# Bulk loads from ScalarE's queue instead of SyncE's, and raw tiles loaded and searched one product later

## The chip, the cores and the metric

The kernel runs on one core of a Trainium2 chip. Its engines are TensorE (PE in the profile; PEld is its weight load), VectorE (DVE), ScalarE (ACT), GpSimd (POOL) and SyncE (SP), which only issues transfers. An engine takes its instructions in order and waits for semaphores of the others. A transfer is issued by an instruction of SyncE, ScalarE or GpSimd and moved by 16 DMA engines. The metric is the device time of one execution in microseconds.

## What is computed

Two independent parts, whose results stand side by side in the output: a causal attention with a sliding window of 256 (2048 tokens, 32 heads of 32), and an FNet mixing layer, the real part of a two-dimensional DFT written as products with DFT matrices.

```
def _A_ref(x, wqkv, wo):
    H = 32; Dh = D // H; W = 256
    q, k, v = ...
    scores = jnp.einsum("bhqd,bhkd->bhqk", q, k) * (Dh ** -0.5)
    mask = (idx[:, None] - idx[None, :] >= 0) & (idx[:, None] - idx[None, :] < W)
    p = _softmax(jnp.where(mask[None, None], scores, -1e9), axis=-1)
    ...
    return o @ wo
def _B_ref(x, dft_seq_re, dft_seq_im, dft_hid_re, dft_hid_im):
    a = jnp.einsum("bsd,ed->bse", x, dft_hid_re)
    b = jnp.einsum("bsd,ed->bse", x, dft_hid_im)
    return jnp.einsum("ts,bse->bte", dft_seq_re, a) - jnp.einsum("ts,bse->bte", dft_seq_im, b)
```

## The kernel before

All inputs are float32. To multiply them on TensorE in float16, each tile is scaled by a power of two and split into a high and a low half; a product of two split tiles is three passes of matmuls (`PASSES`). The scale comes from a search over the raw tile (its largest value, or a sum of absolute values), and a small matmul (`pt_...`, L183) spreads the result over the partitions.

**Stages.** First the projections q, k and v (matmuls pq, pk, pv of 128x512), whose results go to a scratch tensor in HBM (qk, vs). From about 140 us on, the attention runs between the matmuls of everything else: 256 blocks of 128 queries, each with scores (s, far), an exponential on ScalarE (L278), a split (L281, L282), a DMA transpose on SyncE (L284), and the product with v (pv). The generator `attention` is stepped by `tick`, at a rate given by tables, so the attention is spread evenly over the matmuls.

From about 565 us on come four rounds of 12 units. In a round the first four units ("x") multiply the DFT over the hidden axis: their left operand lies in HBM as ready sums and differences (xs), which `x_left` loads as un_a, un_b, un_c and a quarter "t" into `spare`, a part of reg1. The other eight units ("c") multiply the DFT matrix of the sequence axis: `u_load` loads two raw float32 tiles (raw_u, 512 KB each), `u_top` searches them on ScalarE (L786), `u_scale` spreads the scale (pt_u), and `u_step` splits and combines them into un_a, un_b, un_c and a part of reg1. A unit is one call of `seven`: a Strassen-like scheme with seven products of 12 matmuls, accumulated in three PSUM banks in the order "abacaba". After product 0 ScalarE copies bank a to bank c (L1084); after the others ScalarE copies a bank out (L1053) or VectorE adds it (L1055). Names p_a, p_b, p_c are these banks. The last stage multiplies the attention's output with wo (po_a, po_b, po_c).

**What sets the order.** The program is written out in one order; a scheduler then orders each engine's instructions by the times it expects, and `tc.issue_after(i)` forbids it to put an instruction before i on the same engine. In the rounds, `do(n, turn, f, ...)` puts work of later units behind product `turn` of unit n. `behind_act[0]` is ScalarE's latest copy out of PSUM, `behind[0]` the latest of VectorE's. Raw tiles rotate through 5 buffers (`rawp`), un_a, un_b, un_c through 4 (`stp`), the attention's qk tiles through 2.

**Loads.** Every load goes out from SyncE, in one line with the stores and the transposes. `do_load` (L230) loads the q and k of one group and chunk of the attention, two blocks before a chunk ends, or at its first use. `u_load` (L777; the first two units of a round go through `load`, L216) loads the raw tiles of unit n behind products 1 and 5 of unit n - 3; `u_top` searches them behind products 0 and 2 of unit n - 2, `u_scale` follows behind product 6. `x_left` (L806, L811) loads the left sums of unit n behind products 0, 3 and 4 of unit n - 1.

Of the kernel before, what the change touches and what calls it, by code (L numbers as in the profile page):

```python
# [15 lines left out]
AF = mybir.ActivationFunctionType  # L16
# [37 lines left out]
def fused_kernel(ctx: ExitStack, tc: tile.TileContext, xa, wqk, wv, wo, xb, wd, cs, out):  # L54
# [92 lines left out]

    marks = []

    def top(key, raw, i, n):  # L150

        if i == 0:
            tops[key] = small.tile([P, n], F32, tag=f"top{n}", name=f"top_{key}")
        with tc.issue_after(behind[0].ins) if behind else nullcontext():
            vec(nc.vector.tensor_reduce, tops[key][:, i:i + 1], raw, axis=AX.XY, op=ALU.max,
                apply_absolute_value=True)

    def mean(key, raw, i, n):
# [59 lines left out]
    def attention():  # L218
# [6 lines left out]

        def do_load(g, hp, sc):
            if (g, hp, sc) in q2s:
                return
            u = att.tile([96, 2, 2, CH], F16, tag="qk", name=f"qk_{g}_{hp}_{sc}")
            nc.sync.dma_start(u.rearrange("p h a t -> p (h a t)"), qk[g, sc, :, :, 2 * hp:2 * hp + 2]  # L230
                              .rearrange("j d h a t -> (j d) (h a t)"))
            q2s[g, hp, sc], k2s[g, hp, sc] = u[:, :, 0], u[:, :, 1]
# [10 lines left out]
        def s_step(b, j):  # L243
# [33 lines left out]
            for h in range(2):  # L277
                nc.scalar.activation(sv[:, h], sv[:, h], AF.Exp, bias=bias[:, h:h + 1], scale=es)  # L278
            hl = att.tile([P, 8 * P], F16, tag="hl", bufs=3, name=f"hl_{b}")
# [72 lines left out]
        for b in range(nblk + LAG):  # L352
            for j in range(2):
# [16 lines left out]
                if j == 1 and b < nblk and blocks[b][3] == 1 and b + 3 < nblk:  # L370
                    g, hp, sc, _ = blocks[b + 3]
                    if (g, sc) in ready:
                        do_load(g, hp, sc)
                if j == 1 and b < nblk and blocks[b][3] == 3 and b + 1 < nblk:
# [398 lines left out]
    def u_load(n, j=0):  # L773
        if n < len(units):
            kind, p, c, i = units[n]
            raws[n, j] = rawp.tile([P, ND, P], F32, tag="raw", name=f"raw_u{n}_{j}")
            (load if i < 2 else nc.sync.dma_start)(raws[n, j], cs[p, 2 * i + j, :, 8 * c:8 * c + 8])  # L777

# [19 lines left out]
    def x_left(n, step):  # L798

        _, _, c, k = units[n]  # L800
        src = xs[4 * c + k]
        u = uns.setdefault(n, {})
        part = lambda t, k0: (lambda h, d: t[:, h, k0 + d])
        if step == "t":
            t = spare[:, k % 2 * 8 * P:(k % 2 + 1) * 8 * P]
            nc.sync.dma_start(t, src[:, 6 * HP:])  # L806
            u[5] = part(t.rearrange("p (h k t) -> p h k t", h=2, k=4), 0)
            return
        j, held_by = {"a": (0, (0, 3)), "c": (1, (6, 4)), "b": (2, (2, 1))}[step]
        t = stp.tile([P, 2, ND, P], F16, tag="st", name=f"un{n}_{step}").rearrange("p h d t -> p (h d t)")  # L810
        nc.sync.dma_start(t, src[:, 2 * j * HP:2 * (j + 1) * HP])  # L811
        for k, pos in enumerate(held_by):
            u[pos] = part(t[:, k * HP:(k + 1) * HP].rearrange("p (h d t) -> p h d t", h=2, d=4), 0)
# [292 lines left out]
    with tc.tile_pool(name="pb", bufs=1) as pb:  # L1106
# [14 lines left out]
        for r in range(4):  # L1121
# [8 lines left out]
            for j in range(8):  # L1130
                n = c0 + j
                do(n - 3, 1, u_load, n, 1)
                do(n - 3, 5, u_load, n, 0)
                do(n - 2, 0, u_top, n, 1)
                do(n - 2, 2, u_top, n, 0)
                do(n - 2, 6, u_scale, n)
                for step, turn in enumerate((0, 1, 1, 2, 3, 4)):
                    do(n - 1, turn, u_step, n, step)
# [125 lines left out]
```

## Time and profile before

| | us |
|---|---|
| median of three runs (1696.62 to 1700.1) | 1697.67 |
| profiled execution | 1697.51 |
| its span, first to last instruction | 1695.7 |

The busy time of every engine in 40 equal slices of the span (tenths; 9 is 90% or more), the mean busy share of the 16 DMA engines, and below it the part of the page on DMA queues:

```profile
PE   9999999999999999999999999999999999999999
PEld 4444545554555554555554555545555545444444
DVE  7657888888888689887688896688886698687442
ACT  4476666677877687887687886687887688563322
POOL 0000222334434341444423475433565425411000
DMA  6678999999999994887998999986999977866431
...
q1 hardware_dynamic: 462064, 321.48, 75.9%
q0 software_dynamic: 7680, 25.17, 9.0%
```

A row of a group of instructions reads: line, engine, operation, what it writes, what it reads, how often, busy time, mean duration in ns, idle time before it and what ended that. A row of waits reads: who waited for whom, total us, times, longest us.

### The profile page before, as it was taken

To read this page: it belongs to the slowest core of one execution; us is meant where nothing else is said; L and a number is where in the kernel's file an instruction comes from. 1 tells how busy PE (TensorE), PEld (TensorE's weight loads), DVE (VectorE), ACT (ScalarE), POOL (GpSimd) and SP (SyncE) were. 2 spreads that over 40 slices of the span, in tenths; PEclk is the share of its full clock that TensorE was granted. 3 is DMA by queue.
4 is the path that set the end of the run, shared out by engine and by line. 5 is a ranking of instruction groups with operands and counts; after the bars stand their busy time and mean duration, and the time that the engine had idled before them with its cause. 6 is when DMAs were issued, how large, how long until landed. Compare 5 with 4: busy or idle time off the path is not lost.

```text
span 1695.7 us, 30919 instructions
## 1 busy us (share of the span) xinstructions
PE 1687.6 (100%) x11007; PEld 846.6 (50%) x11007; DVE 1304.8 (77%) x2256; ACT 1169.8 (69%) x2035; POOL 571.0 (34%) x812
## 2 busy tenths in 40 slices
PE   9999999999999999999999999999999999999999
PEld 4444545554555554555554555545555545444444
DVE  7657888888888689887688896688886698687442
ACT  4476666677877687887687886687887688563322
POOL 0000222334434341444423475433565425411000
DMA  6678999999999994887998999986999977866431
GB/s 246 239 269 246 248 289 285 279 259 303 245 234 222 208 225 122 205 200 171 232 245 250 196 182 182 230 200 120 193 183 203 227 181 140 174 184 120 116 99 75
DMA packets 469898, 348.62 MB, mean 206 GB/s; under 512 B 376944, under 2 KB 409968, under 8 KB 468848
## 3 DMA queue, kind: packets, MB, share of 16 engines
q1 hardware_dynamic: 462064, 321.48, 75.9%
q0 software_dynamic: 7680, 25.17, 9.0%
q8 instruction: 86, 1.41, 0.3%
q14 instruction: 68, 0.56, 0.1%
HBM read 166.99 MB, written 106.17 MB: 161 GB/s over the span
## 4 chain that ended last, share of the span: by engine, by line
PE 83%; ACT 4%; DMA 4%; DVE 3%; issue 3%; POOL 2%; SPq 0%; POOLq 0%; ACTq 0%; DVEq 0%
PE p_a L119 23%; PE pv L119 12%; PE p_b L119 11%; PE pk L119 9%; PE pq L119 9%; PE p_c L119 6%; PE po_a L119 5%; PE s L119 3%; PE po_b L119 2%; PE far L119 1%; PE po_c L119 1%; DMA o<-ohl 1%; POOL z L296 1%; ACT s L278 1%; POOL t L298 1%
## 5 line engine op out<-in xcount | busy, mean ns | idle before, releaser
L278 ACT ACTIVATE s<-s,bias,escs 128x256 f32<-128x256 f32 (+1 forms) x512 | 270.1, 528 | 11.7
L296 POOL TENSOR_SCALAR_AFFINE_SELECT z<-t 128x512 f16<-128x512 f16 x224 | 183.1, 825 | 190.0 <-PE pv L119 167.2
L275 POOL TENSOR_SCALAR bias<-bias 128x1 f32<-128x1 f32 x128 | 53.5, 418 | 548.0 <-ACT bias L272 405.3
L272 ACT ACTIVATE bias<-mx,pshift,escs 128x2 f32<-128x2 f32 x256 | 98.4, 384 | 165.4 <-DVE mx L269 164.4
L282 DVE TENSOR_TENSOR hl<-s,hl 128x512 f16<-128x512 f32 (+1 forms) x256 | 169.8, 664 | 50.4 <-ACT hl L281 49.9
L119 PEld LDWEIGHTS <-reg 128*128 128x128 f16 x1344 | 128.7, 97 | 141.6
L298 POOL TENSOR_SCALAR_AFFINE_SELECT t<-t 128x512 f16<-128x512 f16 x224 | 188.1, 848 | 11.6
L119 PE MATMUL p_a<-reg,un_c 128*128 128x512 f16 x768 | 181.4, 379 | 0.5 <-DVE reg L859 0.3
L119 PE MATMUL pk<-reg,wu_k 128*128 128x512 f16 x768 | 174.3, 379 | 0.0
L269 DVE TENSOR_REDUCE mx<-s 128x2 f32<-128x512 f32 (+1 forms) x256 | 170.7, 667 | 3.4
L119 PE MATMUL pv<-reg,reg 128*128 128x512 f16 x768 | 172.5, 379 | 0.0
L119 PEld LDWEIGHTS <-un_c 128*128 128x128 f16 x1152 | 109.9, 97 | 121.8 <-issue 2.4
L119 PEld LDWEIGHTS <-un_b 128*128 128x128 f16 x1152 | 109.4, 97 | 117.4 <-issue 0.7
L119 PEld LDWEIGHTS <-un_a 128*128 128x128 f16 x1152 | 109.4, 97 | 116.5
L119 PE MATMUL pq<-reg,wu_q 128*128 128x512 f16 x696 | 156.3, 379 | 0.0
L281 ACT ACTIVATE hl<-s 128x512 f16<-128x512 f32 (+1 forms) x256 | 148.8, 581 | 5.5
L119 PE MATMUL p_a<-reg,un_b 128*128 128x512 f16 x576 | 136.4, 379 | 0.1
L119 PE MATMUL p_c<-reg,un_a 128*128 128x512 f16 x576 | 136.5, 379 | 0.0
L119 PE MATMUL p_b<-reg,un_b 128*128 128x512 f16 x576 | 136.3, 379 | 0.1
L119 PE MATMUL p_a<-reg,un_a 128*128 128x512 f16 x576 | 136.2, 379 | 0.0
L267 DVE COPY_PREDICATED s<-upper,far 128x256 f32<-128x256 uint32 x224 | 94.3, 421 | 51.6 <-PE s L119 50.6
L119 PEld LDWEIGHTS <-qk 96*128 96x128 f16 x1056 | 87.6, 97 | 63.6 <-DMA qk<-qk 2.2
(217 smaller groups left out, 3136.6 us busy)
## 6 DMA issues: line engine op xcount, KB each, us to landing
raw_u<-in_cs_dram SPq DMA_DIRECT2D x64, 512.0 KB, 4.8
qk<-qk SPq DMA_DIRECT2D x64, 384.0 KB, 4.8
out_dram<-y POOLq DMA_DIRECT2D x72, 256.0 KB, 6.2
raw_wd<-in_wd_dram SPq DMA_DIRECT2D x24, 512.0 KB, 5.6
vs<-yv SPq DMA_DIRECT2D x32, 264.0 KB, 4.1
vt<-vs SPq DMA_DIRECT2D x64, 132.0 KB, 3.5
qk<-yq SPq DMA_DIRECT2D x32, 256.0 KB, 4.0
raw_wo<-in_wo_dram SPq DMA_DIRECT2D x16, 512.0 KB, 8.6
```

Source lines behind the costliest of these rows:

```text
L119: fixed[:] = [nc.tensor.matmul(*args, **kwargs)]
L267: nc.vector.copy_predicated(s[:, :, P:], upper2, d["far"] if nb == 3 else never2)
L269: nc.vector.tensor_reduce(mx, sv, axis=AX.X, op=ALU.max, negate=True)
L272: nc.scalar.activation(bias[:, :2], mx, AF.Identity, bias=pshift, scale=es)
L275: marks[:] = [nc.gpsimd.tensor_scalar(bias[:, 2:3], bias[:, 0:1], 1.0, None, op0=ALU.mult)]
L278: nc.scalar.activation(sv[:, h], sv[:, h], AF.Exp, bias=bias[:, h:h + 1], scale=es)
L281: nc.scalar.activation(hi, sv, AF.Copy)
L282: behind[:] = [nc.vector.tensor_tensor(lo, sv, hi, op=ALU.subtract)]
L296: nc.gpsimd.affine_select(out=z, in_=pk, compare_op=ALU.is_gt, fill=0.0, base=0, pattern=[[0, 4], [-1, P]], channel_multiplier=1)
L298: nc.gpsimd.affine_select(out=pk, in_=pk, compare_op=ALU.is_ge, fill=0.0, base=0, pattern=[[0, 4], [1, P]], channel_multiplier=-1)
```

## The change

The 64 raw tiles of the rounds, the 64 left sums, and those 60 of the 64 q and k loads that are issued ahead go out from ScalarE's queue. A new function `bulk` issues a load on ScalarE behind the latest copy out of PSUM. The q and k loads go behind the last Exp of the block before the latest one (`behind_exp[0]`). Raw tiles are loaded behind products 2 and 6 instead of 1 and 5, and searched behind products 1 and 3 instead of 0 and 2. The loads of v, all stores and all transposes stay on SyncE.

```diff
+    def bulk(dst, src):
+        with tc.issue_after(behind_act[0].ins) if behind_act else nullcontext():
+            nc.scalar.dma_start(dst, src)
...
-        def do_load(g, hp, sc):
+        def do_load(g, hp, sc, queue=None):
...
-            nc.sync.dma_start(u.rearrange("p h a t -> p (h a t)"), qk[g, sc, :, :, 2 * hp:2 * hp + 2]
-                              .rearrange("j d h a t -> (j d) (h a t)"))
+            with tc.issue_after(behind_exp[0].ins) if queue else nullcontext():
+                (queue or nc.sync).dma_start(u.rearrange("p h a t -> p (h a t)"), qk[g, sc, :, :, 2 * hp:2 * hp + 2]
+                                             .rearrange("j d h a t -> (j d) (h a t)"))
...
-                nc.scalar.activation(sv[:, h], sv[:, h], AF.Exp, bias=bias[:, h:h + 1], scale=es)
+                e = nc.scalar.activation(sv[:, h], sv[:, h], AF.Exp, bias=bias[:, h:h + 1], scale=es)
+            behind_exp[:] = behind_exp[-1:] + [e]
...
-                        do_load(g, hp, sc)
+                        do_load(g, hp, sc, nc.scalar)
...
-            (load if i < 2 else nc.sync.dma_start)(raws[n, j], cs[p, 2 * i + j, :, 8 * c:8 * c + 8])
+            bulk(raws[n, j], cs[p, 2 * i + j, :, 8 * c:8 * c + 8])
...
-            nc.sync.dma_start(t, src[:, 6 * HP:])
+            bulk(t, src[:, 6 * HP:])
...
-        nc.sync.dma_start(t, src[:, 2 * j * HP:2 * (j + 1) * HP])
+        bulk(t, src[:, 2 * j * HP:2 * (j + 1) * HP])
...
-                do(n - 3, 1, u_load, n, 1)
-                do(n - 3, 5, u_load, n, 0)
-                do(n - 2, 0, u_top, n, 1)
-                do(n - 2, 2, u_top, n, 0)
+                do(n - 3, 2, u_load, n, 1)
+                do(n - 3, 6, u_load, n, 0)
+                do(n - 2, 1, u_top, n, 1)
+                do(n - 2, 3, u_top, n, 0)
```

Line numbers of the changed kernel are 4 to 6 higher. Three places in the built order show what moves. The first is around the load of the q and k of group 1, second pair of heads, first chunk (qk_1_1_0). On SyncE before, where t is a transpose, o the attention's output, and qk_57 the scratch tensor that q and k are stored to and read from:

```order
L240 DMA vt_1_0_3_4245<-vs_58 128x4x132
L284 DMA_TRANSPOSE t_44_4283<-hl_44_4280 128x8x128
L349 DMA_TRANSPOSE o_1_0_1_4155<-ohl_1_0_1_4322 128x4x128
L911 DMA qk_57<-yq4_3_4340 128x2x512
L912 DMA qk_57<-yq4_3_4340 128x512
L230 DMA qk_1_1_0_4395<-qk_57 96x2048
L912 DMA qk_57<-yk4_0_4422 128x512
```

On ScalarE in the changed kernel, where the junk row is the search of a raw weight tile:

```order
L352 ACTIVATE ohl_1_0_1_4322<-o_1_0_1_4155 128x256
L913 ACTIVATE yq4_3_4340<-pq4_3_4257 128x512
L167 ACTIVATE junk_100,top_wq5_4345<-raw_wq5_4192 128x1024
L235 DMA qk_1_1_0_4395<-qk_57 96x2048
L277 ACTIVATE bias_45_4377<-mx_45_4375,pshift_95,escs_118 128x2
L283 ACTIVATE s_45_4369<-s_45_4369,bias_45_4377,escs_118 128x256 x2
```

The load leaves SyncE's line of transposes and stores and stands between a search and the next block's bias on ScalarE.

The second place is unit 7, a c unit, behind its products 1 and 2, on ScalarE before (s, bias, hl are the attention's; y0 and reg1 on the left of p2_7 are copies out of banks; un8 and u9 belong to the next two units):

```order
L1053 ACTIVATE y0_6682<-p2_7_b_8599,sc_u7_8295 128x512
L132 ACTIVATE reg1_83<-raw_u8_1_8077,sc_u8_8591 128x512
L278 ACTIVATE s_111_8646<-s_111_8646,bias_111_8654,escs_118 128x256 x2
L281 ACTIVATE hl_111_8659<-s_111_8646 128x512
L272 ACTIVATE bias_112_8702<-mx_112_8700,pshift_95,escs_118 128x2
L1053 ACTIVATE y0_6682<-p2_7_a_8598,sc_u7_8295 128x512
L786 ACTIVATE junk_100,top_u9_8668<-raw_u9_0_8558 128x1024
```

The same place in the changed kernel:

```order
L1059 ACTIVATE y0_6682<-p2_7_b_8599,sc_u7_8293 128x512
L132 ACTIVATE reg1_83<-raw_u8_1_8130,sc_u8_8589 128x512
L792 ACTIVATE junk_100,top_u9_8688<-raw_u9_1_8428 128x1024
L277 ACTIVATE bias_111_8654<-mx_111_8652,pshift_95,escs_118 128x2
L277 ACTIVATE bias_112_8700<-mx_112_8698,pshift_95,escs_118 128x2
L283 ACTIVATE s_111_8646<-s_111_8646,bias_111_8654,escs_118 128x256
L1059 ACTIVATE y0_6682<-p2_7_a_8598,sc_u7_8293 128x512
L160 DMA raw_u10_1_8759<-in_cs_dram 128x1024
L283 ACTIVATE s_112_8694<-s_112_8694,bias_112_8700,escs_118 128x128
```

The search of the first tile of unit 9 now stands here instead of that of the second, and the load of a tile of unit 10 stands behind the copy of product 2.

The third place is TensorE at the end of unit 4 (p2_4; un4_b is its left operand, s and qk the attention's), as one piece of the difference:

```order
 L119 MATMUL s_100_7942<-qk_3_0_1_7637 128x128
-L183 LDWEIGHTS top1_u6_7892
-L183 MATMUL pt_u6_7980<-unit_85,top1_u6_7892 128x128
 L119 LDWEIGHTS un4_b_7716
 L119 MATMUL p2_4_a_7785<-reg1_83,un4_b_7716 128x512
@@ -8343,4 +8341,6 @@
 L119 LDWEIGHTS un4_b_7716
 L119 MATMUL p2_4_a_7785<-reg1_83,un4_b_7716 128x512
+L187 LDWEIGHTS top1_u6_7908
+L187 MATMUL pt_u6_7978<-unit_85,top1_u6_7908 128x128
 L119 LDWEIGHTS un5_a_7801
 L119 MATMUL p2_5_a_7986<-reg1_83,un5_a_7801 128x512
```

The matmul that spreads the scale of unit 6 moves from ahead of unit 4's last product to behind it. This happens to 13 of the 32 pt_u; the other matmuls keep their order.

More of the change, by code (lines that the diff above doesn't have):

```diff
@@ L146, in fused_kernel @@
     behind = []
-    marks = []
+    marks, behind_exp = [], []
     def top(key, raw, i, n):
```

## The prediction

> **What bounds the kernel now.** I read the page's busy times first, then TensorE's waits, then the chain of waits, to see how much of the span is not matmul at full rate.
>
> ```profile
> PE 1687.6 (100%) x11007; PEld 846.6 (50%) x11007; DVE 1304.8 (77%) x2256; ACT 1169.8 (69%) x2035; POOL 571.0 (34%) x812
> ...
> PE s L119 <- DMA qk<-qk: 1.5, 1, 1.5
> PE wps L744 <- DVE reg L736: 1.2, 1, 1.2
> PE pq L119 <- DMA wx<-in_xa_dram: 0.6, 1, 0.6
> PE p_a L119 <- ACT y L1053: 0.4, 1, 0.4
> PE p_a L119 <- DVE y L1055: 0.3, 1, 0.3
> PE p_a L119 <- DVE reg L859: 0.3, 1, 0.3
> PE p_a L119 <- ACT p_c L1084: 0.2, 1, 0.2
> ```
>
> The first line is busy time by engine, the others are all of TensorE's waits (total, times, longest). TensorE is busy for 1687.6 of 1695.7 us. It waits 4.5 us in all, of which 1.8 us lie in the start (wps, pq), which the change does not touch. What a change of loads can give back here is 2.7 us: 1.5 us in one wait for a q and k load, and 1.2 us in four small waits for ScalarE and VectorE in the rounds.
>
> Busy is not the same as full rate, so I check the rate:
>
> ```profile
> L119 PE MATMUL p_a<-reg,un_c 128*128 128x512 f16 x768 | 181.4, 379 | 0.5 <-DVE reg L859 0.3 <-ACT p_c L1084 0.2
> ...
> 1521.51 2.59 PE p_a L119 x12
> ```
>
> One matmul is shown for 379 ns, but the chain of waits has 12 of them, one product, in 2.59 us, 216 ns each. A gap shorter than 379 - 216 = 163 ns is therefore not seen as a wait. Nearly every product in the chain has the same 2.59 us, so I take it that little hides there. The kernel is at TensorE's rate; the change removes no matmul, and the order of TensorE differs only in 13 of the 32 pt_u matmuls. A gain is bounded by about 2.7 us of 1697; a loss is not bounded in that way.
>
> **The change part by part.** First, the q and k loads. The wait of 1.5 us stands here (SyncE's queue, then TensorE, then ScalarE, in order of time; last two of the page's rows of issues, which end in us to landing):
>
> ```profile
> 394.17 0.38 SPq L911 DMA_DIRECT2D qk<-yq  x1
> ...
> 399.92 1.83 SPq L284 DMA_TRANSPOSE t<-hl  x1
> 401.85 1.21 SPq L349 DMA_TRANSPOSE o<-ohl  x1
> 403.16 0.54 SPq L911 DMA_DIRECT2D qk<-yq  x1
> 403.75 0.46 SPq L912 DMA_DIRECT2D qk<-yq  x1
> 404.30 0.39 SPq L230 DMA_DIRECT2D qk<-qk  x1
> ...
> 408.87 0.28 PE L119 MATMUL s<-qk 96*128 96x128 f16 x2 [1.52 <-DMA qk<-qk]
> ...
> 393.46 0.57 ACT L907 ACTIVATE yq<-pq 128x512 f16<-128x512 f32 x1
> 393.92 1.05 ACT L163 ACTIVATE junk<-raw_wq 128x1024 uint8<-128x1024 f32 x1
> 394.87 0.19 ACT L163 ACTIVATION_READ_ACCUMULATOR junk<-raw_wq 128x1 f32 x1
> 396.34 0.39 ACT L272 ACTIVATE bias<-mx,pshift,escs 128x2 f32<-128x2 f32 x1 [1.28 <-DVE mx L269]
> ...
> qk<-qk SPq DMA_DIRECT2D x64, 384.0 KB, 4.8
> ...
> qk<-yq SPq DMA_DIRECT2D x32, 256.0 KB, 4.0
> ```
>
> The load of qk_1_1_0 is issued at 404.30, behind transposes and stores, and TensorE stood 1.52 us for it. In the new order it stands on ScalarE right behind the search of raw_wq5, which ends at 395.06. Issued there, with 4.8 us to landing, it lands near 400, 9 us ahead of 408.87. It may first have to wait for a store of q such as the one issued at 394.17, with 4.0 us to landing: then it goes out near 398 and lands near 403, still in time. ScalarE would stand for some 2 us past 396.34, where VectorE held it already. **Term: -1.5 us.** Next late there is nothing that the waits show; the other loads of q and k caused no listed wait. Those that SyncE issued early now go out later, behind an Exp, but still two to three blocks ahead of use.
>
> Second, what 188 issues (60 of qk, 64 raw tiles, 64 left sums) cost on ScalarE. The trace has no issue on ScalarE; on SyncE they take (min/median/max in ns):
>
> ```profile
> L230 SPq DMA_DIRECT2D qk<-qk x64: 319/498/1600, 122.6 to 1415.4; - x64
> L777 SPq DMA_DIRECT2D raw_u<-in_cs_dram x48: 327/338/1226, 629.3 to 1487.9; - x48
> L811 SPq DMA_DIRECT2D un_a<-xs x16: 319/460/1740, 529.8 to 1354.1; - x16
> L806 SPq DMA_DIRECT2D reg<-xs x16: 319/332/2195, 559.7 to 1350.8; - x16
> ```
>
> With these medians: 60 x 0.498 + 64 x 0.338 + 48 x 0.460 + 16 x 0.332 = 79 us of sequencer time. Below, the cost is nothing: ScalarE's rows above overlap (the yq copy ends at 394.03, the search starts at 393.92), so its sequencer is at the next instruction while one still runs, and an issue of 0.34 to 0.50 us fits under an ACTIVATE of 0.54 to 1.05 us. Above, it is all 79 us. I take a value near the lower end, since the overlap is shown on ScalarE itself. What covers the rest is idle time of ScalarE, 1695.7 - 1169.8 = 526 us over the span, most of it waits that a later start shortens:
>
> ```profile
> ACT bias L272 <- DVE mx L269: 97.6, 77, 4.2
> ...
> 592.00:640.00 48.00, 47.54 (x322) 23.79 (x321) 41.53 (x72) 40.94 (x76) 18.08 (x28) 1.00 0.86 212
> 688.00:800.00 112.00, 112.00 (x858) 59.32 (x856) 94.42 (x177) 96.02 (x178) 49.79 (x75) 1.00 0.83 192
> 840.00:888.00 48.00, 47.99 (x340) 24.59 (x338) 39.64 (x70) 38.22 (x73) 16.39 (x24) 1.00 0.95 222
> ```
>
> The first row is ScalarE's wait for mx in 592 to 1490; the others are stretches with busy time of PE, PEld, DVE, ACT, POOL. In 688 to 800 (matrix units) ScalarE has 16 us idle; six units bring 12 raw issues and about 5 of qk, 12 x 0.338 + 5 x 0.498 = 6.5 us. In 592 to 640, where a round goes from left sums to matrix units, 7.1 us are idle, and up to 7 issues per unit (four left sums, two raw, one qk), 17 in 2.5 units, are 7 us at 0.42: there the cover would be used up. What waits behind a late ScalarE are the copies that free TensorE's banks:
>
> ```profile
> L1084 ACT ACTIVATE p_c<-p_a x48: 553/582/626, 564.5 to 1532.0; 128x512 f32<-128x512 f32 x48
> L1053 ACT ACTIVATE y<-p_a,sc_u x48: 657/687/690, 655.2 to 1537.1; 128x512 f32<-128x512 f32 x48
> ```
>
> TensorE comes back to a bank one product (2.59 us) after leaving it; a copy takes 0.58 or 0.69 us, so ScalarE may be 1.9 to 2.0 us late before TensorE stands. The new raw loads stand behind such a copy, at products 2 and 6, with the next urgent one two products on. **Term: +0.3 us**, a quarter on top of the 1.2 us of waits in the rounds; the ends are -1.2 us (those waits go) and the second rival below.
>
> Third, waits that move with the loads. SyncE waited for the raw tiles' buffers:
>
> ```profile
> SPq L777 <- DVE un_c L126: 33.4, 13, 4.1
> SPq L777 <- DVE un_b L126: 20.9, 13, 2.3
> ```
>
> On ScalarE such a wait would hold everything behind it. But the loads go one product later, 2.59 us plus the attention in it: the 2.3 us is covered, the 4.1 us all but 1.5 us at its worst. I take 0; the end above is 1.5 us. SyncE loses 188 issues, and its transposes come earlier; TensorE has no wait for t or vt in the list, so that is worth 0.
>
> Fourth, the search one product later. It is the same work (un_c is the split beside it):
>
> ```profile
> L786 ACT ACTIVATE junk<-raw_u x64: 1040/1047/1067, 607.4 to 1501.4; 128x1024 uint8<-128x1024 f32 x64
> L786 ACT ACTIVATION_READ_ACCUMULATOR junk<-raw_u x64: 185/192/214, 608.4 to 1502.3; 128x1 f32 x64
> L132 ACT ACTIVATE un_c<-raw_u,sc_u x32: 1136/1144/1159, 638.9 to 1524.2; 128x1024 f16<-128x1024 f32 x32
> L126 DVE TENSOR_REDUCE top_u<-top_u x32: 99/144/155, 618.7 to 1502.8; 128x1 f32<-128x2 f32 x32
> L126 DVE TENSOR_SCALAR top_u<-top_u x32: 105/145/154, 618.9 to 1503.5; 128x1 uint32<-128x1 uint32 x32
> ```
>
> From product 3's end to pt_u behind product 6 are three products, 7.8 us. In them ScalarE does the copy (0.69), un_c (1.14) and the search (1.05 + 0.19), and VectorE 0.14 + 0.15 us: 3.4 us, and 4.4 us are left for what the queues hold. I take 0.
>
> **Sum.** The profiled execution took 1697.51 us, 1.8 us more than its span and 0.16 us under the median of 1697.67. 1697.5 - 1.5 + 0.3 = **1696.3 us**.
>
> One rule of the Trainium skill speaks against more than this: DMA: Bandwidth & Descriptors, in Issuing engines are not separate DMA queues, says that DMAs started by ScalarE, SyncE or GpSimd run on the same 16 DMA engines and interleave, and that starting them on several engines saves only issue time. By it the 4.8 us to landing stay and the sum is the same; no run here shows a queue of ScalarE.
>
> **The rivals.**
> 1. The loads come no earlier where it matters, or the wait turns up at another load: SyncE's place in line at 404.30 speaks against it, the loads of qk that now go out later speak for it. The 1.5 us come back: 1697.5 to 1697.8 us.
> 2. Slower: ScalarE runs out of idle time where a round goes from left sums to matrix units (592 to 640, 840 to 888, and twice more). If each issue costs its full 0.42 us there, 7 us meet 7.1 us of idle of which perhaps half can be used; 3.5 us late, less the 1.9 us that a copy allows, is 1.6 us of stall, and at two or so urgent copies per stretch 3.2 us: 4 x 3.2 = 13 us, 1709 us. At half that price, 1702.5 us. It decides as soon as an issue keeps ScalarE itself for more than about 0.3 us. For it: 85% busy in 592 to 640. Against: the overlap of instructions.
> 3. pt_u holds TensorE: the 4.4 us left are eaten by exponentials in front. At 0.1 us for each of 32 it is 3 us, 1699.5 us. The order moves 13 of the pt_u back, up to a product, which speaks against it.
> 4. Faster by over 0.2%: all 2.7 us go, and gaps under 163 ns besides: 1694 us.
>
> **How the numbers follow.** My forecast (1695.5 to 1697.2) has 0.47, rival 1 0.12, rival 3 0.13, rival 2 0.20 and rival 4 0.08. A measurement of this kernel tells about 0.2%, 3.4 us, from no change: same is 1694.3 to 1701.1 us. The forecast and rivals 1 and 3 are all within it, 0.72; rival 2 is slower, rival 4 faster. The range leaves out the far part of rival 2 and reaches to the edge of rival 4: 1694.0 to 1704.0 us.
>
> **What would show it.** Right: no wait of s for qk near 408; TensorE's listed waits at 3 to 4 us; ScalarE's instructions next to an issue with no gap of 0.3 us. Wrong: TensorE waits for y L1053 or p_c L1084 that add up to several us at 592 to 660 and 880 to 910 (rival 2), waits of pt_u for top_u (rival 3), or a wait for qk at another block (rival 1).

## The result and the profile after

| | us |
|---|---|
| before, median over the four runs beside it (1696.62 to 1704.37) | 1698.88 |
| after, median (1757.72, 1768.51, 1769.49, and one run of 6327.7) | 1769.0 |
| profiled execution after (span 1767.4) | 1769.49 |
| ratio after / before | 1.0386, 95% interval 1.0328 to 1.0443 |

The change is slower by 3.9%; the forecast was 1696.3 us. Here and below a ratio leaves out runs that are over 1.5% slower than the fastest of the same kernel, such as the one of 6327.7 us, which nothing here explains.

From the page of the changed kernel, the busy times, and TensorE's granted clock in 40 slices of the span. Its line numbers are 4 to 6 higher than before: L1084 is now L1090, L1053 is L1059, the transposes' L284 is L290.

```profile
PE 1701.3 (96%) x11007; PEld 849.9 (48%) x11007; DVE 1308.7 (74%) x2256; ACT 1171.4 (66%) x2035; POOL 561.5 (32%) x812
...
PEclk9999999999999999999999998999999899999999
```

The list of TensorE's waits after, its three largest rows (total us, times, longest):

```profile
PE p_a L119 <- ACT p_c L1090: 19.5, 4, 15.1
PE p_b L119 <- DMA un_b<-xs: 17.5, 1, 17.5
PE pv L119 <- DVE sc_u L126: 9.9, 1, 9.9
```

All 15 rows of that list add up to 62.7 us, where before they had 4.5: 58.2 us of new waits. TensorE's busy time is 1701.3 - 1687.6 = 13.7 us longer for the same 11007 matmuls. Together that is 71.9 us, and the span grew by 71.7. So all of it is TensorE standing, and TensorE running slower. Three stalls (17.5, 15.1 and 9.9 us, 42.5 in all) make most of it: in this execution it is not a small cost per load but a few accidents.

What TensorE waits for differs from stall to stall, but ScalarE's own new waits name one thing, the late transposes. Two rows of its list, of the kernel after:

```profile
ACT hl L287 <- DMA t<-hl: 41.6, 10, 21.1
ACT s L283 <- DMA t<-hl: 19.6, 2, 17.6
```

The tile view of t, after: the DMA transposes that bring the exponentials from hl into t, with the duration of their issue (min/median/max in ns, first and last start) and their time to landing:

```profile
L290 SPq DMA_TRANSPOSE t<-hl x256: 1188/1312/18765, 147.2 to 1522.4; - x128
...
DMA to landing us min/median/max: 2.7/5.4/34.7
```

The same rows of the kernel before:

```profile
L284 SPq DMA_TRANSPOSE t<-hl x256: 1188/1254/6185, 147.1 to 1453.5; - x128
...
DMA to landing us min/median/max: 2.4/4.6/13.0
```

The median moved by 0.8 us, the longest from 13.0 to 34.7 us. Counted in the same records, 2 of 256 transposes took over 10 us before, and 31 after. ScalarE's next write into hl needs the transpose of three blocks ago, and ScalarE works in order, so everything that it does for TensorE stands behind that write. The third stall (9.9 us, ending at 973.9) came this way: ScalarE stood 8.2 us for hl until 967.4, and the scale sc_u was late behind it.

The largest stall came another way: TensorE waited for a left sum itself, while ScalarE stood for hl beside it. The timeline of the kernel after, of SyncE, ScalarE and TensorE in turn (start, duration, engine, line, operation; in brackets the idle time before it and what ended it):

```profile
1076.14 33.44 SPq L290 DMA_TRANSPOSE t<-hl  x3
...
1077.07 0.33 ACTq L160 DMA_DIRECT2D un_b<-xs  x1
1079.98 0.33 ACTq L160 DMA_DIRECT2D un_c<-xs  x1
1085.50 0.34 ACTq L160 DMA_DIRECT2D un_a<-xs  x1
1085.88 0.45 ACTq L160 DMA_DIRECT2D reg<-xs  x1
1110.92 0.60 ACT L287 ACTIVATE hl<-s 128x512 f16<-128x512 f32 x1 [21.13 <-DMA t<-hl]
...
1086.50 1.89 PE L119 MATMUL p_a<-reg,un_a 128*128 128x512 f16 x8
1105.88 1.89 PE L119 MATMUL p_b<-reg,un_b 128*128 128x512 f16 x4 [17.49 <-DMA un_b<-xs]
1108.60 3.36 PE L119 MATMUL p_b<-reg,un_b 128*128 128x512 f16 x8
```

And the same place of the program before, all on SyncE:

```profile
1072.79 0.53 SPq L811 DMA_DIRECT2D un_b<-xs  x1
1074.99 0.32 SPq L811 DMA_DIRECT2D un_c<-xs  x1
1075.40 7.95 SPq L284 DMA_TRANSPOSE t<-hl  x2
1083.44 0.53 SPq L806 DMA_DIRECT2D reg<-xs  x1
1084.09 1.22 SPq L811 DMA_DIRECT2D un_a<-xs  x1
```

The four left sums go out at nearly the same pace in both kernels (within 11.3 us before, 8.8 after). Before, two transposes behind un_b and un_c were issued in 8 us; after, three took 33 us, and un_b itself, issued at 1077.07, landed 28.8 us later. Both streams suffer.

In the packet records a transpose is 1024 pieces of 256 bytes and a left sum or raw tile 128 pieces of 4 KB. The slowest transpose of the kernel before, issued at 898.7, stood in line for 9.3 us, and then its 1024 pieces went through in 2.9 us. In the kernel after, in the ten us from 1086 on, 455 pieces of transposes, 291 large pieces of ScalarE's queue and 127 of GpSimd's stores were moved side by side: a transpose no longer stands in line, and goes at a fraction of its pace. The rate of all queues fell too: with SyncE's line full the kernel before moved 399 GB/s from 890 to 908 us, the kernel after 133 in the stall and 49 from 1100 to 1110. Why the packets take so long there is open.

The second stall, of 15.1 us, came by way of a load's issue (SyncE, ScalarE, TensorE in turn):

```profile
1358.01 21.23 SPq L290 DMA_TRANSPOSE t<-hl  x3
...
1366.10 0.39 ACT L277 ACTIVATE bias<-mx,pshift,escs 128x2 f32<-128x2 f32 x1 [0.20 <-DVE mx L274]
1383.76 0.33 ACTq L160 DMA_DIRECT2D reg<-xs  x1
1384.14 1.11 ACT L283 ACTIVATE s<-s,bias,escs 128x256 f32<-128x256 f32 x2 [17.65 <-DMA t<-hl]
...
1385.77 0.59 ACT L1090 ACTIVATE p_c<-p_a 128x512 f32<-128x512 f32 x1
...
1386.42 1.01 PE L119 MATMUL p_a<-reg,un_b 128*128 128x512 f16 x2 [15.06 <-ACT p_c L1090]
```

In this program the transfers of SyncE and of ScalarE count their landings on the same eight semaphores, and in both kernels no issue starts before the transfer that used its semaphore last has landed (all 1119 pairs in each trace). The issue of reg takes the semaphore of the transpose issued at 1358.01, which landed at 1383.74. So the 17.6 us in the row of s above are not the exponential's wait: a moved load stood on ScalarE for a late transpose, 17.3 us long, and the copy p_c that TensorE needs stood behind it. Idle time of this kind, before an issue of ScalarE's own, adds up to 24.2 us in the change, 18.9 of it for transposes.

The last row of the first timeline shows where the other 13.7 us come from: 8 matmuls in 3.36 us against 1.89 before the stall. The stretches around it (us, busy time of PE, PEld, DVE, ACT, POOL, then the granted clock, DMA share, GB/s; a share over 1 means that packets' times overlap):

```profile
1087.00:1105.00 18.00, 1.39 (x7) 0.42 (x5) 0.82 (x2) 1.87 (x4) 0.07 (x1) 0.61 1.24 133
1105.00:1115.00 10.00, 9.12 (x54) 4.42 (x55) 2.45 (x5) 2.20 (x5) 2.68 (x5) 0.67 1.23 120
1115.00:1130.00 15.00, 15.00 (x102) 7.62 (x101) 7.77 (x13) 9.23 (x17) 6.78 (x11) 1.00 1.20 168
```

After the stall the granted clock is 0.67 over 10 us, then 1.00 again: a long stall is paid twice. The Trainium skill, TensorE: Matmul & The Clock Gate (Part 1: The HAM clock gate), says that an idle window of about 3.4 us halves the array's clock until the array has again been busy for about as long; the rows agree in kind, with matmuls at about half pace behind the stall, but a mean of 0.67 over 10 us is half the clock for 6.6 of them, longer than that window.

### The profile page after: what moved, and what is told of

It reads as the page before. It is cut to its first block, busy times and chain, and to the rows that moved or that the text cites. A ratio compares the mean times of both kernels' runs of the same rounds, so it can differ in the third digit from the quotient of the medians.

```text
span 1767.4 us, 30831 instructions
## 1 busy us (share of the span) xinstructions
PE 1701.3 (96%) x11007; PEld 849.9 (48%) x11007; DVE 1308.7 (74%) x2256; ACT 1171.4 (66%) x2035; POOL 561.5 (32%) x812
## 4 chain that ended last, share of the span: by engine, by line
PE 74%; DMA 11%; DVE 6%; ACT 4%; issue 3%; POOL 1%; ACTq 0%; SPq 0%; DVEq 0%; POOLq 0%
PE p_a L119 19%; PE pv L119 13%; PE p_b L119 9%; PE pq L119 9%; PE pk L119 8%; DMA t<-hl 7%; PE p_c L119 5%; PE po_a L119 5%; PE s L119 2%; PE po_b L119 2%; DMA un_b<-xs 2%; PE po_c L119 1%; PE far L119 1%; DVE reg L865 1%; DMA out_dram<-y 1%
## 5 line engine op out<-in xcount | busy, mean ns | idle before, releaser
L302 POOL TENSOR_SCALAR_AFFINE_SELECT z<-t 128x512 f16<-128x512 f16 x224 | 178.7, 805 | 256.7 <-PE pv L119 154.7
L280 POOL TENSOR_SCALAR bias<-bias 128x1 f32<-128x1 f32 x128 | 45.7, 357 | 559.1 <-ACT bias L277 416.9
L119 PE MATMUL p_a<-reg,un_b 128*128 128x512 f16 x576 | 141.5, 389 | 24.8 <-ACT p_c L1090 19.5
L119 PE MATMUL p_b<-reg,un_b 128*128 128x512 f16 x576 | 138.6, 384 | 19.4 <-DMA un_b<-xs 17.5
```

The costliest lines, as they stand in the source:

```text
L119: fixed[:] = [nc.tensor.matmul(*args, **kwargs)]
L280: marks[:] = [nc.gpsimd.tensor_scalar(bias[:, 2:3], bias[:, 0:1], 1.0, None, op0=ALU.mult)]
L302: nc.gpsimd.affine_select(out=z, in_=pk, compare_op=ALU.is_gt, fill=0.0, base=0, pattern=[[0, 4], [-1, P]], channel_multiplier=1)
```

## The experiments

Theory Q: with two hardware queues (SyncE's transposes, ScalarE's bulk copies), the transposes land late, ScalarE waits for them in order, TensorE for ScalarE. (That the bulk loads themselves land late, as in the largest stall, is no part of it; the wait at an issue was read from the traces and has no run of its own.) Rivals: C, the later search and load do the harm; I, ScalarE's issues do it; M, it is bytes, whatever the queue. Ratios are to the kernel before, run on the same chip, with their 95% intervals, from 3 to 10 runs; the last two columns are of one profiled execution each (in e2_qk the slowest of its ten, 1709.5 us).

| label | what differs from before | ratio | longest t<-hl, us | over 10 us, of 256 |
|---|---|---|---|---|
| (before) | | 1 | 13.0 | 2 |
| e15_few | 128 additional issues of 8 KB on ScalarE | 1.0002 (0.9986 to 1.0018) | 13.1 | 4 |
| e2_qk | qk on ScalarE | 1.0008 (0.9991 to 1.0024) | 17.0 | 12 |
| e1_turns | turns | 1.0041 (1.0029 to 1.0053) | 11.7 | 2 |
| e7_dose_act | 64 additional copies of 512 KB on ScalarE | 1.0110 (1.0086 to 1.0135) | 18.6 | 9 |
| e3_raw | turns, raw tiles on ScalarE | 1.0111 (1.0053 to 1.0169) | 20.6 | 13 |
| e8b_dose_sp | the 64 additional copies on SyncE | 1.0114 (1.0088 to 1.0141) | 17.0 | 9 |
| e4_left | left sums on ScalarE | 1.0146 (1.0094 to 1.0198) | 23.6 | 17 |
| e5_small | the change in 512-byte pieces | 1.0202 (1.0143 to 1.0262) | 15.9 | 18 |
| e13_two | raw tiles and left sums on ScalarE | 1.0219 (1.0195 to 1.0243) | 26.3 | 28 |
| e11_mild | e13_two in 512-byte pieces | 1.0226 (1.0181 to 1.0271) | 13.7 | 15 |
| e10_noqk | the change, qk on SyncE | 1.0255 (1.0216 to 1.0294) | 24.8 | 27 |
| e14_t5 | the change, 5 t buffers | 1.0296 (1.0232 to 1.0359) | 22.6 | 22 |
| e9_queues | the change, old turns | 1.0369 (1.0320 to 1.0418) | 30.3 | 32 |
| (after) | the change | 1.0386 (1.0328 to 1.0443) | 34.7 | 31 |
| e6_hl4 | the change, 4 hl and 5 t buffers | 1.0473 (1.0425 to 1.0522) | 30.3 | 39 |

Over these 16 profiled executions the last column goes with the span (correlation 0.96; 1695.7 us with 2, 1724.2 with 13, 1748.2 with 27, 1776.5 with 39 late transposes), more closely than the longest one does (0.89). That is a correlation and no proof. Two runs stand outside the table, e8_dose_sp and e12_tiny, and are told below.

### Which part of the change: e1, e2, e3, e4, e9, e10, e13

The first four take one part each of the change. e1_turns, the turns alone (the other loads and the search alike):

```diff
-                do(n - 3, 1, u_load, n, 1)
+                do(n - 3, 2, u_load, n, 1)
...
```

e2_qk, qk alone:

```diff
-                        do_load(g, hp, sc)
+                        do_load(g, hp, sc, nc.scalar)
```

e3_raw, the turns and the raw tiles:

```diff
-            (load if i < 2 else nc.sync.dma_start)(raws[n, j], cs[p, 2 * i + j, :, 8 * c:8 * c + 8])
+            bulk(raws[n, j], cs[p, 2 * i + j, :, 8 * c:8 * c + 8])
```

e4_left, the left sums alone:

```diff
-            nc.sync.dma_start(t, src[:, 6 * HP:])
+            bulk(t, src[:, 6 * HP:])
...
-        nc.sync.dma_start(t, src[:, 2 * j * HP:2 * (j + 1) * HP])
+        bulk(t, src[:, 2 * j * HP:2 * (j + 1) * HP])
```

> The kernel before with only the turns moved: raw tiles loaded and searched one product later, every load still issued by SyncE. Theory Q (two queues: bulk copies of ScalarE's queue and SyncE's DMA transposes hold each other up on the DMA engines, ScalarE then waits for an hl buffer and TensorE for ScalarE): no second queue here, so within 0.3% of before (1695 to 1703 us), transposes of t<-hl landing in 4.6 us by the median and 13 at most. Rival C (the later search and load alone make the scale or a left sum late): most of the 70 us is here already, 1750 us or more, with TensorE waits for un or for the copies and a longest transpose as before.

> The kernel before with only the 60 qk loads of the blocks on ScalarE's queue. They come in 1 KB pieces and 23 MB. Theory Q with the harm from large packets (4 KB, of raw tiles and left sums): 1695 to 1699 us, the 1.5 us wait of s for qk gone, transposes landing at most 15 us late. Rival L (any load on ScalarE's queue couples the two issuing engines, whatever its size): over 1715 us. Rival C: as before.

> The kernel before with the turns moved and the 64 raw tiles (512 KB in packets of 4 KB) on ScalarE's queue, left sums and qk on SyncE. Theory Q: 25 to 45 us of the 70 (1722 to 1745 us), transposes of t<-hl landing up to 20 us and more. Rival B (the harm needs raw tiles and left sums in flight together, that is more than one bulk load at a time): under 1707 us. Rival C: the same as e1.

> The kernel before with only the 64 loads of left sums (48 of 512 KB in packets of 4 KB, 16 of 256 KB) on ScalarE's queue, turns as before. They come in bursts of three and four at a round's product. Theory Q: 25 to 45 us of the 70 (1722 to 1745 us), with the longest transposes where the burst stands. Rival B: under 1707 us. Rival C: as before, 1695 to 1703 us.

The turns alone cost 0.41%, 7 us, more than theory Q allowed them and far from rival C's 50. qk alone costs nothing that can be measured. Raw tiles (1722.6 us, of which the turns are 7) and left sums (1726.8 us) each cost a part, at the lower end of what theory Q expected, so one kind of bulk load at a time is enough to cost time. In e4_left TensorE's longest wait is one for qk, which SyncE issues in line with the late transposes:

```profile
PE far L119 <- DMA qk<-qk: 12.3, 1, 12.3
```

The parts add up to 0.41 + 0.08 + 0.70 + 1.46 = 2.65%, less than the 3.86% of the whole; by the intervals the difference of 1.2 is uncertain by about 1.0. Three further kernels are the change with parts put back: e9_queues has the old turns, e10_noqk has qk on SyncE, e13_two both. The two edits, against the changed kernel:

```diff
-                do(n - 3, 2, u_load, n, 1)
+                do(n - 3, 1, u_load, n, 1)
...
-                        do_load(g, hp, sc, nc.scalar)
+                        do_load(g, hp, sc)
```

> The changed kernel with the old turns: raw tiles, left sums and qk on ScalarE's queue, loads and search one product earlier again. If the parts add up (turns 7 us by the run with the turns alone): 1757 to 1765 us. If the later search makes the late loads worse (the parts alone give 45 of 70 us, so some 25 are left over): 1735 to 1752 us. Rival C again (the turns are what hurts): under 1710 us.

> The changed kernel with qk back on SyncE: raw tiles and left sums on ScalarE's queue, turns moved. qk alone cost 1.4 us at most. If the parts add up: 1765 to 1770 us. If the pieces of qk in the second queue stand between the 4 KB pieces and lengthen the time in which transposes meet them: 1735 to 1760 us. qk on SyncE then stands behind late transposes, as in the runs with raw tiles or left sums alone (TensorE waited 2 to 12 us for qk there), so it can also be over 1770 us.

> Raw tiles and left sums on ScalarE's queue in their 4 KB pieces, qk on SyncE, old turns: the control of the run with 512-byte pieces (2.26% over before, longest transpose 13.7 us). By the sum of the parts (2.55% without qk, less 0.4% for the turns): 1728 to 1740 us, with transposes of 20 us and more. If small pieces gain here as they did in the full change: 1745 us or more. If it is within 5 us of the run with small pieces, then these took the transposes' lateness away and gave the time back through ScalarE's 256 issues.

e9_queues (1759.5 us) and the change itself can't be told apart by their intervals; e13_two (1738.0) is what its parts say. qk, worth nothing alone, is worth 1.3 to 1.5% on top of the others (3.86 against 2.55, and 3.69 against 2.19 with the old turns). A load that is harmless alone is not harmless in a queue that already hurts.

### Bytes or issues: e7, e8, e8b, e12, e15

These add work to the kernel before, from which nothing is read, and move no load. e7_dose_act:

```diff
+    extra = [tc.dram_tile((P, ND, P), F32, name=f"extra{k}") for k in range(64)]
...
             (load if i < 2 else nc.sync.dma_start)(raws[n, j], cs[p, 2 * i + j, :, 8 * c:8 * c + 8])
+            with tc.issue_after(behind_act[0].ins) if behind_act else nullcontext():
+                nc.scalar.dma_start(extra.pop(), cs[p, 2 * i + j, :, 8 * c:8 * c + 8])
```

> The kernel before, with 64 additional copies of 512 KB (each raw tile once more, from its place in memory to a scratch place in memory that nothing reads) issued by ScalarE at the raw tile's load. Nothing waits for them, and all loads stay on SyncE. Theory Q: transposes land up to 15 to 25 us late and the kernel takes 1712 to 1745 us, since the interleaving alone does the harm. Rival W (the harm is that the moved loads themselves come late): within 0.3% of before, 1695 to 1704 us.

1717.2 us: no load comes from another queue, and still 1.1% goes, with transposes up to 18.6 us. Its control put the same copies on SyncE:

```diff
+            (load if i < 2 else nc.sync.dma_start)(extra.pop(), cs[p, 2 * i + j, :, 8 * c:8 * c + 8])
```

> The same 64 additional copies issued by SyncE, behind the raw tile's load in the same queue: the same bytes, no second hardware queue. Theory Q: a copy stands in line ahead of the next transpose for 2 to 4 us, so transposes land at most some 15 us late and the time is 1697 to 1710 us, less than with the copies on ScalarE's queue. Rival M (the bytes do it: memory or DMA engines are full): as much as with ScalarE's queue, 1712 to 1745 us.

This one measured something else. Nothing held 48 of the 64 copies in place, and the scheduler put them at the program's start: the first transpose was issued at 198.8 us instead of 147.2, and the kernel took 1753.6 us, 54 more than before, of which 51.6 are in that start. e8b_dose_sp holds each copy behind the latest ordered load or transpose of SyncE:

```diff
+            with tc.issue_after(line[0].ins):
+                nc.sync.dma_start(extra.pop(), cs[p, 2 * i + j, :, 8 * c:8 * c + 8])
```

> The 64 additional copies on SyncE's queue once more, now each held behind the last ordered load so that it stands beside its raw tile's load in the rounds (in the run before, 48 of them went to the program's start). Same bytes as with the copies on ScalarE's queue (1717.2 us), no second hardware queue. Theory Q: 1697 to 1710 us, and no more than a third of the additional time of the copies on ScalarE's queue; longest transpose 17 us or less. Rival M (the bytes alone do it): 1712 to 1725 us, the same as with ScalarE's queue.

1719.8 us, the same as on ScalarE's queue: here rival M is right and my expectation wrong. Bytes added in front of the transposes cost, whichever queue they stand in. To see what is left of a difference I fitted, for each run, the 256 landing times against what was under way when the transpose was issued (a least-squares fit of my own over the trace's issues and landings, a correlation and no proof; such a fit explains 64% of the spread before and 36% after, and other choices of terms move its slopes by up to 0.2 us):

| run | 512 KB under way in SyncE's queue | 512 KB in ScalarE's | 256 KB of stores in GpSimd's |
|---|---|---|---|
| before | +1.0 us (1.47 under way by the mean) | | +1.2 us (0.33) |
| e7_dose_act | +1.2 (1.52) | +1.6 us (0.26) | +1.4 (0.35) |
| e8b_dose_sp | +1.2 (1.84) | | +1.5 (0.39) |
| e4_left | +1.1 (1.22) | +2.1 (0.29) | +1.8 (0.34) |
| e13_two | +1.1 (1.01) | +1.7 (0.61) | +2.0 (0.35) |
| after | +0.9 (0.79) | +1.9 (0.73) | +2.4 (0.39) |

By the fit a copy in the other queue holds a transpose up 1.3 to 2.1 times as long as one in its own. In e7 the dose on ScalarE gives 0.26 x 1.6 = 0.42 us per transpose; in e8b the additional 1.84 - 1.47 = 0.37 of a copy on SyncE give 0.37 x 1.2 = 0.44. So the fit has the two cost about the same: copies in the own queue cost less each, but more of them are under way. In the change the bytes are unchanged: 0.68 of a copy left SyncE's queue (0.68 x 0.9 = 0.6 us back), and 0.73 came to ScalarE's (0.73 x 1.9 = 1.4 us).

Rival I needs the issues without the bytes. e12_tiny adds 128 copies of 128 rows of 4 bytes where the change issues its raw tiles and left sums; e15_few the same with 16 rows of 512 bytes. The edit of e15_few, in which e12_tiny has `cs[p, 2 * i + j, :, 8 * c, 0:1]` and `src[:, :2]`:

```diff
+    extra = [tc.dram_tile((16, 256), F16, name=f"extra{k}") for k in range(128)]
...
+    def tiny(src, dt=F16):
+        with tc.issue_after(behind_act[0].ins) if behind_act else nullcontext():
+            nc.scalar.dma_start(extra.pop().bitcast(dt), src)
...
+            tiny(cs[p, 2 * i + j, 0:16, 8 * c], F32)
...
+            tiny(src[0:16, :256])
...
+        tiny(src[0:16, :256])
```

> The kernel before with 128 additional tiny copies (128 rows of 4 bytes from memory to a scratch place that nothing reads) issued by ScalarE where the changed kernel issues its raw tiles and left sums; all real loads stay on SyncE. So ScalarE pays the issues and the DMA engines get next to no bytes. Theory Q: 1697 to 1704 us, transposes of t<-hl landing within 15 us. Rival I (the issues on ScalarE are the cost, by delaying its copies): 1715 us or more, with TensorE waiting for p_c and y.

> As the run with the 128 tiny copies, but each copy is 16 rows of 512 bytes (16 pieces, 8 KB) instead of 128 rows of 4 bytes: the same 128 issues at the same places of ScalarE, an eighth of the pieces. Theory Q: 1697 to 1704 us, transposes of t<-hl landing within 15 us by the median 4.6 to 4.8, and p_c and y on time. Rival I (the issues on ScalarE are the cost): 1712 us or more. If any copy on the second queue slows the DMA engines by itself, as the 4-byte copies did: over 1730 us with transposes of 20 us.

e12_tiny took 2031.3 us, 1.1968 (1.1937 to 1.1999) times before. Taken alone that is what rival I expected, with TensorE's largest waits for y (59.1 us) and p_c (57.0 us); but its transposes were late too, so it is no test of issues alone, and is told with the hardware below. e15_few is one. Its largest row of TensorE's waits:

```profile
PE s L120 <- ACT hl L286: 1.5, 1, 1.5
```

And, from the tile view of t, the landing of its transposes:

```profile
DMA to landing us min/median/max: 2.4/4.6/13.1
```

128 issues on ScalarE cost nothing (1.0002), though they take 72.0 us of its sequencer, and the transposes land as before. So the time of the issues is not the cost, and rival I falls as it was put: what costs is what the copies bring. An issue costs where it must stand for a late transfer, as the one at 1383.76 in the change; in e15_few, where transfers are on time, ScalarE stands 4.1 us in all before its issues.

### How the lateness passes on: e6, e14

```diff
-            hl = att.tile([P, 8 * P], F16, tag="hl", bufs=3, name=f"hl_{b}")
+            hl = att.tile([P, 8 * P], F16, tag="hl", bufs=4, name=f"hl_{b}")
...
-            t = att.tile([P, 8, P], F16, tag="t", bufs=6, name=f"t_{b}")
+            t = att.tile([P, 8, P], F16, tag="t", bufs=5, name=f"t_{b}")
```

> The changed kernel with 4 hl buffers instead of 3, and for the room 5 t buffers instead of 6. Theory Q passes the lateness on through ScalarE, which waits in order for the hl buffer that the transpose three blocks back still reads: one buffer more covers one block's time more, so 1715 to 1750 us, with ACT hl <- DMA t<-hl well under the 41.6 us of the changed kernel. Rival T (TensorE waits for the late left sums or t themselves, whatever ScalarE does): 1760 to 1775 us.

> The changed kernel with 5 t buffers instead of 6 and its 3 hl buffers: the control of the run with 4 hl buffers (1783 us). Theory Q through ScalarE's wait for hl: 1785 to 1810 us, so that the fourth hl buffer is worth some us. If the fourth hl buffer gains nothing and the wait only moves (in that run to ohl <- o): 1775 to 1790 us. If t buffers cost nothing: 1765 to 1772 us, and the fourth hl buffer made it worse.

Both expectations failed. With 4 hl buffers the time was 1783.2 us; with only the t buffer taken away 1756.5, under all three expectations. By the ratios (1.0473 against 1.0296) the fourth hl buffer made it worse by 1.8%, some 30 us; the missing t buffer alone did no harm that the intervals show (1.0296 against the change's 1.0386). Two of ScalarE's waits in e6_hl4:

```profile
ACT bias L277 <- DVE mx L274: 145.6, 127, 4.3
ACT ohl L352 <- POOL o L349: 88.1, 36, 22.7
```

The wait for hl has left the top of the list, and the wait of ohl for o (the block's output, which needs the products with t) has grown from 36.1 us, longest 4.2, to 88.1, longest 22.7. So the hl buffer was only the first place where ScalarE met the late transpose: given a buffer, it stands at the next instruction that needs the same transpose. Why that costs some 30 us more is open.

### Smaller pieces: e5, e11

Both cut the bulk copies of ScalarE's queue into rows of 512 bytes, e5_small in the changed kernel and e11_mild in e13_two:

```diff
     def bulk(dst, src):
         with tc.issue_after(behind_act[0].ins) if behind_act else nullcontext():
-            nc.scalar.dma_start(dst, src)
+            for k in range(2):
+                nc.scalar.dma_start(dst[:, k::2], src[:, k::2])
...
-        bulk(t, src[:, 2 * j * HP:2 * (j + 1) * HP])
+        bulk(t.rearrange("p (k e) -> p k e", e=256), src[:, 2 * j * HP:2 * (j + 1) * HP].rearrange("p (k e) -> p k e", e=256))
```

> The changed kernel with the bulk copies of ScalarE's queue cut into pieces of 512 bytes instead of 4 KB: each raw tile or left sum goes as two copies, of its even and of its odd rows of 512 bytes, so the bytes and the queue stay and the pieces are 8 times as many. Theory Q by pieces (the DMA engines take a piece from each queue in turn, so a 256-byte piece of a transpose waits for one 4 KB piece): transposes of t<-hl land within 15 us, and the kernel takes 1700 to 1725 us. Rival S (the two queues share bytes, or any traffic of a second queue holds a transpose, or the issuing engines are coupled): no better than the changed kernel, 1755 us or more, with transposes of 20 us and above.

> Everything at once that made the changed kernel milder: raw tiles and left sums on ScalarE's queue in pieces of 512 bytes, qk on SyncE, old turns. Theory Q (dose and piece size): the run without qk had 2.55% over before, the turns are worth 0.4 of these, and small pieces took away about half (3.86% to 2.02%), so 0.9 to 1.4% over before, 1714 to 1723 us, with no transpose of t<-hl over 16 us. Rival P (small pieces only helped because qk's 1 KB pieces stood in the same queue): 1730 to 1740 us. A version with loads on a second queue that beats before would be under 1697 us, which no theory here expects.

In e5_small the longest transpose falls from 34.7 to 15.9 us and the time from 1769.0 to 1731.6 us, between the two theories. In e11_mild the longest falls from 26.3 (e13_two) to 13.7 us, as theory Q by pieces has it, but the time stays: 1737.2 against 1738.0, and my 1714 to 1723 was wrong. One reason can be seen in ScalarE's timeline of e11_mild:

```profile
1086.82 0.54 ACT L284 ACTIVATE s<-s,bias,escs 128x256 f32<-128x256 f32 x1 [1.47 <-PE pv L119]
1086.85 2.14 ACTq L161 DMA_DIRECT2D un_c<-xs  x1
1089.03 0.54 ACT L284 ACTIVATE s<-s,bias,escs 128x256 f32<-128x256 f32 x1 [1.67 <-issue]
```

and the largest row of TensorE's waits there is:

```profile
PE p_a L119 <- ACT p_c L1091: 17.2, 12, 6.4
```

A copy in 512-byte pieces can take ScalarE 2.14 us to issue, and ScalarE stands meanwhile ("issue"). Adding up ScalarE's idle time under its own issues, where nothing else ended it, gives 24 us in e11_mild, 2.6 in e13_two, 4.8 in the change; before its issues, standing for earlier transfers, it is idle for another 24.7 us in e11_mild and 7.1 in e13_two. The p_c row fits that. The small pieces took the transposes' tail away and the issues, twice as many, gave time back; whether that is the whole of it is not settled.

## Why the prediction was wrong

- **The wait for qk goes (-1.5 us): right in its place.** No wait of s for qk stands in the list after. The load went out at 397.8 us and landed at 403.5, as worked out. The gain drowned in the rest; e2_qk, which does this part alone, measures no change.
- **The issues on ScalarE (+0.3 us): right for their time.** The issues cost 47.4 us (128 of L160) and 20.0 us (60 of qk), 67 us of sequencer time where I had worked out 79, and ScalarE's instructions run on above them; e15_few shows that 128 of them cost nothing. The second rival, ScalarE out of idle time, is not what happened: TensorE did wait for p_c and y, as that rival's sign had it, but because ScalarE stood for transposes, at hl or at an issue, and the longest of these from 1371 us on, not where that rival put it.
- **The third step failed, twice.** Of a wait that moves to ScalarE with a load it says: "On ScalarE such a wait would hold everything behind it." That came true, but the step priced only the waits for the raw tiles' buffers and took 0. The wait that came was for a semaphore that a late transpose had used: 17.3 us on ScalarE, 15.1 us of TensorE's stalls. And of the transposes it says: "SyncE loses 188 issues, and its transposes come earlier; TensorE has no wait for t or vt in the list, so that is worth 0." The transposes came later, up to 34.7 us, and the moved queues without the turns (e9_queues) cost 3.69 of the 3.86%. That TensorE has no wait for t says only that t was early enough while all traffic stood in one line; it is no price for what happens when the line is split. With it fell the sentence that the landing of 4.8 us stays: by the median it does (raw_u 5.2 us after, qk 4.9), but un_b took 28.8 us (the stall of 17.5 us), 31 of 256 transposes took over 10 us, and the time goes with such late transfers, not with the median.
- **The rule that I weighed, and the one that I left out.** Issuing engines are not separate DMA queues, in the Trainium skill's DMA: Bandwidth & Descriptors, says that the copies interleave on the same engines. I read it as no change; the word that counted was "interleave". Of the same page, Queues, rings and completion order states that each DMA engine goes round the queues that have work, a packet at a time. By it a long transpose of many small pieces gives up its turn to bulk copies in a second queue, which in one queue it did not; the packet records agree in that pieces of both kinds are moved side by side (455 and 291 in the ten us from 1086 on), though they don't show the turns of one engine.
- **A view of the trace before would have shown it.** GpSimd's stores were already a second queue. Counted in the packet records of before, from 520 us on, the 122 transposes with no large piece of that queue started while they were under way landed in 4.1 us by the median, the 12 with 128 pieces or more in 7.8 us. I looked for what ScalarE's queue would cost in the rows of ScalarE, and the answer stood in GpSimd's.
- **The search one product later (0): mis-sized.** e1_turns has it at 0.41%, 7 us. TensorE's waits there add up to 11.6 us against 4.5 before, in twelve small ones, the largest row for y (2.8 us in four). The third rival, pt_u holding TensorE, has next to nothing of it: in the changed kernel the wait of pt_u is 0.3 us and those for top_u 2.4.
- **The bound of the loss.** I wrote that a loss is not bounded as a gain is, and then ended the range at 1704 us with only ScalarE's own load as a price. No rival had a late transfer, or one passed on by an engine that works in order.

None of the kernels beats the one before. With 4.5 us of waits in it, none of these changes could have won more than the 2.7 us of the prediction.

## What to carry to other kernels

Before a load is moved to another engine's queue, look at what it stood behind: one queue in order is also a schedule, in which here the bulk copies and the short transfers that the pipeline waits for stood behind each other. Read the landing time of those short transfers by how many are late and by what was under way in other queues, since an engine that works in order pays for the late ones, and TensorE pays again at a lower clock. Ask, too, which semaphore a moved load's issue has to wait for, since on an engine that also computes everything stands behind that wait. And try each part of such a change alone as well as together: here the parts add up to 2.65% and the whole is 3.86%.

## What the hardware showed unexpectedly

The tiny copies of e12_tiny (128 rows of 4 bytes each, 128 copies, 0.07 MB in all) cost 331 us. Its queues of SyncE and ScalarE, its landings, and the landings of e15_few's copies, 8 KB each in 16 pieces:

```profile
q1 hardware_dynamic: 462064, 321.48, 85.9%
...
q10 hardware_dynamic: 18432, 0.07, 1.1%
...
t<-hl SPq DMA_TRANSPOSE x256, 7.2
extra<-xs ACTq DMA_DIRECT2D x64, 0.5 KB, 10.8
```

```profile
q10 hardware_dynamic: 4096, 1.06, 0.3%
...
t<-hl SPq DMA_TRANSPOSE x256, 4.6
extra<-xs ACTq DMA_DIRECT2D x64, 8.0 KB, 4.5
```

Half a kilobyte took 10.8 us to land and made the transposes beside it slower by the median (7.2 us instead of 4.6), while sixteen times the bytes in an eighth of the pieces landed in 4.5 us and hurt nothing. (In e12_tiny the trace tells the landing of only 33 of the 256 transposes and 19 of the 128 copies.) The copies' own packets take 1.1% of the DMA engines' span and don't show this cost; the row of SyncE's queue does: the same packets and bytes as before took 85.9% of 2016.4 us instead of 75.9% of 1695.7, 1.35 times as long. And ScalarE stood 126 us before its own issues there, against 4.1 in e15_few. What in these pieces it is (their number, or their 4 bytes) was not tried.
